# An FFT kernel's opening stage: folding the first batch in place, and lining up TensorE's work on it

## The chip, the cores and the metric

The kernel runs on one core of a Trainium2 chip. The metric is the device time of one execution in microseconds (us), the median of several runs. A core has TensorE (PE; its weight loads are shown apart, as PEld), VectorE (DVE), ScalarE (ACT), GpSimd (POOL) and SyncE (SP). Transfers between the chip's memory and the core's are issued from SP, ACT or POOL and carried by 16 DMA engines.

## The reference

A two-dimensional Fourier transform whose real part is kept, and then a feed-forward layer with the hardswish gate, all in float32:

```
x: (8, 3008, 256)                      # batch, sequence, dimension
X = fft(fft(x, axis=1), axis=2).real   # -> (24064, 256)
h = X @ w_in                           # w_in:  (256, 2048)
g = h * clip(h + 3, 0, 6) / 6
out = g @ w_out                        # w_out: (2048, 256)
```

## The kernel before

The sequence length is 3008 = 47 x 64. The transform over it is done in two stages: a transform over 47 points by matmuls with the table F (stage 1), a trip through device memory that regroups the rows (tiles z, zd and g), and a transform over 64 points by matmuls with the table T (stage 2). The transform over the dimension is folded into w_in. The inner transform uses symmetry: for a real input it needs only the sums and the differences of column d and column 256 - d ("near" and "far" columns, 127 of each; columns 0 and 128 stand alone). Making these sums and differences is the *fold*.

The eight batches are worked in four pairs. For all but the first batch, stage 1 hides beside the feed-forward layer's matmuls, which fill TensorE. The first batch (halves[0], "hb" in the code) has nothing to hide beside: it makes the opening of the kernel, the first 40 us or so, in which the weights are also loaded and split into exponent and mantissa (lines 778 to 818).

The order on each engine is the order in which the program issues its instructions (the schedule is written out by hand); the engines run apart and meet at semaphores. For the first batch that order is as follows.

- **Loads.** SP loads the first piece of w_in (load_w(0), L757). ACT issues F, FI (a table of identities and indices) and the rows of the special slot n2 = 0, which go into a tile first_slot (L196). POOL issues eight gathers (L175), 128 rows of 4 KB each: for each of four groups of slots, m in FIRST = [0, 1, 3, 2], a tile x and its mirrored partner xr, each one *unit* of 4 slots x 256 columns on partitions 0 to 46 and 64 to 110. Behind them on POOL's queue stand C (L934), a part of T (L865) and two pieces of w_out (load_w(2) and (3), L762).
- **Fillers.** keep_awake(n, w) (L871) issues n matmuls of 128 rows x w columns on a zeroed tile Z, whose product nobody reads. Four of 512 columns run first, one of 128 columns stands ahead of the first unit, and one of 128 columns follows each of units 2 to 6 (L961).
- **Units.** For each unit, fold_unit (L201) makes a tile y from the pool ypool, which has two buffers: the edge columns 0 and 128 are copied (L205, on ACT for most units, on DVE for the first and the last), DVE makes the differences (L207) and the sums (L208). Then unit_columns (L332) does four matmuls of 512 columns, one for each quarter of the array (47 x 64 weights each: two halves of rows by two halves of columns, running side by side), and unit_middle (L326) does eight small products of one or two columns for the middle column 128. A float32 matmul stands in the trace as two records, one for each of its passes. In the group m = 3 one quarter takes the special slot by other tables ("alone"), which makes three matmuls of the one; the special slot's rows are copied into the tile x by ACT (L967) first.
- **Evictions.** When both units of a group are accumulated in PSUM, evict_first (L348) copies them into a tile z: the middle columns (L353) and the first half (L354) on ACT, the second half (L355) on ACT for the first two groups and on DVE for the last two. SP (and ACT, for one half of the last group) then issues the DMAs to zd (L367). In the program's order the eviction of one group stands behind the first unit of the next. Behind the first of them SP issues load_w(1), the second piece of w_in.
- **The last unit.** Its fold is done in two steps of two slots each, and its columns in two rounds of four matmuls of 256 columns. DVE's join(0) (L812), which completes the first piece of w_in, is issued behind them, and so is the third group's eviction ahead of them.
- **After the units.** fold_w_in(0) (wps, L848) waits for join(0) and C; the last group is evicted; load_g_half (L435) brings zd back as g; exponent_a(1) and mantissa(1) (L778, L803, L804) wait for load_w(1), exponent_b(1) (ex, L792) follows on TensorE and exponent_c(1) (L795) on ACT, then join(1), fold_w_in(1), and stage 2 (L455). From about 46 us on the feed-forward layer's matmuls fill TensorE.

The clearing of the table T by ACT (clear_table, L904) and the first piece's exponent (L778, L792, L795) run ahead of the units.

Of the kernel before, what the change touches and what calls it, by code (L numbers as in the profile page):

```python
# [7 lines left out]
F32 = mybir.dt.float32  # L8
# [5 lines left out]
AL = mybir.AluOpType  # L14
# [35 lines left out]
N1, N2 = 47, 64  # L50
# [8 lines left out]
def kernel(  # L59
# [10 lines left out]
    nc = tc.nc  # L70
    P = nc.NUM_PARTITIONS
    B, S, D = x.shape
# [6 lines left out]
    PB, PZ = P // 2, 2 * NK1  # L79
    PX = PB + N1 + 1  # L80
    XC = 4
    NS = N2 // 2
    NXC = NS // XC
    NM = NXC // 2
# [13 lines left out]
    ypool = ctx.enter_context(tc.tile_pool(name="ypool", bufs=2))  # L98
# [41 lines left out]
    FIRST = [0, 1, NM - 1, 2]  # L140
# [54 lines left out]
    def load_zero(o, hb, queue):  # L195
        queue.dma_start(out=o, in_=x_pn[hb.b * N1:(hb.b + 1) * N1 + 1, 0, :])  # L196

    def zero_slot(hb):
        return hb.x[NM - 1][PB:PX, XC - 1, :]

    def fold_unit(x, part, steps=(slice(0, XC),), copy=nc.scalar.copy, sine=nc.vector):  # L201
        y = ypool.tile([PX - 1, XC + 1, D], F32, tag="y", name="y")
        n = PX - 1
        for js in steps:
            copy(y[:, js, 0:P + 1:P], x[0:n, js, 0:P + 1:P])  # L205
            far, near = x[0:n, js, D - 1:P:-1], x[0:n, js, 1:P]
            sine.tensor_tensor(y[:, js, P + 1:D], *((far, near) if part else (near, far)), op=AL.subtract)  # L207
            nc.vector.tensor_tensor(y[:, js, 1:P], near, far, op=AL.add)  # L208
        return y

    def fold_half(hb, m, part, eng):
        xt, xr = hb.x[m][0:PX - 1], hb.xr[m][0:PX - 1]
# [90 lines left out]
    def rows(b):  # L303
        return slice(b * PB, b * PB + N1)

    def table(i, b):
        return F[rows(b), i * PB:(i + 1) * PB]
# [8 lines left out]
    def quarters(m, part):  # L316
        for i in range(2):
            for h in range(2):
                alone = m == NM - 1 and h == i == 1
                a = (2 * i, XC - 1 - 2 * i)[part]  # L320
                n = 1 if alone else 2
                yield i, h, slice(0, n), slice(a, a + n) if part == 0 else slice(a, a - n if a >= n else None, -1), False
                if alone:
                    yield i, h, slice(1, 2), slice(XC - 1, XC) if part == 0 else slice(0, 1), True

    def unit_middle(m, part, x, pt):  # L326
        for i, h, js, slots, alone in quarters(m, part):
            t = (1 + part) if alone else (5, 7)[part]
            nc.tensor.matmul(pt[h][i * PB:(i + 1) * PB, js], table(t, h), x[rows(h), slots, P:P + 1],
                             start=part == 0 and not alone, stop=part == 1, skip_group_check=True)  # L330

    def unit_columns(m, part, y, ps, only=None):  # L332
        def product(o, t, h, moving, begin):
            nc.tensor.matmul(o, table(t, h), moving, start=begin, stop=bool(part), skip_group_check=True)  # L334

        for i, h, js, slots, alone in quarters(m, part):
            o = ps[h][i * PB:(i + 1) * PB]
            if alone and only in (None, 1):
                for k, cs in enumerate((slice(0, P + 1), slice(P + 1, D))):
                    product(o[:, js, cs], 1 + part + 2 * k, h, y[rows(h), slots, cs], False)  # L340
            elif not alone and only is None:
                product(o[:, js], (0, 6)[part], h, y[rows(h), slots], part == 0)
            elif not alone:
                for j, slot in zip(range(js.start, js.stop), range(XC)[slots]):
                    if j == only:
                        product(o[:, j:j + 1], (0, 6)[part], h, y[rows(h), slot:slot + 1], False)

    def evict_first(hb, m, ps, pt):  # L348
        k = FIRST.index(m)
        pool, tag = ((zpool, "z"), (zpool, "z"), (apool, "a"), (cpool, "c"))[k]  # L350
        z = pool.tile([PX, 2, 2, D + 1], F32, tag=tag, name="z")
        for h in range(2):
            nc.scalar.copy(z[:, h, :, D:], pt[h][0:PX])  # L353
        nc.scalar.copy(z[:, 0, :, 0:D], ps[0][0:PX])  # L354
        (nc.vector.tensor_copy if k > 1 else nc.scalar.copy)(z[:, 1, :, 0:D], ps[1][0:PX])  # L355
        if not first.zd:
            first.zd[0] = dpool.tile([NG, 2 * KK, 2, NS, D + 1], F32, tag="zd0", name="zd")
        zd = first.zd[0][:].rearrange("g k c (h n) d -> (g k c) h (n d)", h=2)
        n0 = 2 * 4 * KK
        for i in range(2):  # L360
            n = (m * XC + 2 * i) * (D + 1)
            for j in range(PZ // n0):
                dst = zd[j * n0:(j + 1) * n0, :, n:n + 2 * (D + 1)]
                rs = slice(i * PB + j, i * PB + 2 * n0, 2) if j < 2 else slice(i * PB + 2 * n0, i * PB + PZ)
                src = z[rs].rearrange("p h n d -> p h (n d)")
                if j == 0:
                    (nc.scalar if k == NM - 1 and i else nc.sync).dma_start(out=dst, in_=src)  # L367
                else:
                    later.setdefault((j, k), []).append((dst, src))
# [404 lines left out]
    def exponent_a(j, signs=range(2)):  # L774
        top = raw[j][:].bitcast(I16).rearrange("p (n four) -> p n four", four=4)[:, :, 3]
        for i in signs:
            low = PM[j % len(PM)][:, i].bitcast(U8).rearrange("p (n two) -> p n two", two=2)[:, :, 0]
            nc.scalar.activation(low, top, AF.Identity, bias=bias[:, i:i + 1], scale=(1 - 2 * i) / 16.0)  # L778
# [15 lines left out]
    def exponent_c(j):  # L794
        nc.scalar.activation(exs[j].bitcast(I32), exs[j], AF.Identity, scale=2.0 ** 23)  # L795
# [11 lines left out]
    def join(j):  # L807
        kind, n, i = PIECES[j]
        frac, ex = fracs.pop(j), exs.pop(j)
        if kind == "in":  # L810
            o = wpool.tile([P, WB], F32, tag="wi", bufs=4, name="wi")
            nc.vector.tensor_tensor(o[:], frac, ex, op=AL.mult)  # L812
            w[PIECES[j]] = o[:]
            return

        for h, g in enumerate((B21, B22) if i else (B11, B12)):
            f, e = (t.rearrange("p (c q h e) -> h p c q e", c=2, h=2, e=DH)[h] for t in (frac, ex))
            nc.vector.tensor_tensor(block(n, g).rearrange("p c (q e) -> p c q e", e=DH), f, e, op=AL.mult)

    def block(j, i):  # L820
        return G[:, i, 2 * j:2 * j + 2, :]
# [49 lines left out]
    def keep_awake(n, w=2 * TB):  # L871
        ps = ps_d.tile([P, 2 * TB], F32, tag="d", name="awake")
        for i in range(n):
            nc.tensor.matmul(ps[:, 0:w], ones[:], Z[:, 0:w], start=True, stop=True)
# [5 lines left out]
    hb = halves[0]  # L880
# [1 line left out]
    nc.scalar.dma_start(out=F[:], in_=c_stage1[:, 0:8 * PB])  # L882
    nc.scalar.dma_start(out=FI[:], in_=c_stage1[:, 13 * PB:])
    first_slot = qpool.tile([P, 2 * TB], F32, tag="qn", name="first_slot")
    load_zero(first_slot[PB:PX, 0:D], hb, nc.scalar)
    for k, m in enumerate(FIRST):
        take_half(hb, m, *((xpool, "x"), (xpool, "x"), (qpool, "q"), (apool, "a"))[k])
    bias = wpool.tile([P, 2], F32, tag="bias", name="bias")
# [12 lines left out]
    def clear_table(b):  # L901
        r = slice((1 - b) * N2, (2 - b) * N2)
        t = T[r, b].rearrange("p g a k n -> p g (a k n)")
        nc.scalar.copy(t, Z[r].unsqueeze(1).to_broadcast([N2, NG, 2 * TB]))  # L904
# [31 lines left out]
    for j in range(2, 4):  # L936
        load_w(j)
    clear_table(0)
    exponent_a(0)
    mantissa(0)  # L940
    exponent_b(0)
    keep_awake(1, P)
    clear_table(1)
    for k, m in enumerate(FIRST):
        ps, pt = first_banks(m)
        end = k == NM - 1
        for part, tiles in enumerate((hb.x, hb.xr)):
            x = tiles.pop(m)
            if end and part:
                y = fold_unit(x, 1, (slice(1, XC, 2), slice(0, XC, 2)), copy=nc.vector.tensor_copy)  # L950
                evict_first(hb, FIRST[k - 1], *before)
                unit_middle(m, 1, x, pt)
                for j in range(2):
                    unit_columns(m, 1, y, ps, only=j)
                join(0)
                continue
            y = fold_unit(x, part, copy=nc.scalar.copy if k + part else nc.vector.tensor_copy)
            unit_columns(m, part, y, ps)
            unit_middle(m, part, x, pt)
            if k + part and not end:  # L960
                keep_awake(1, P)  # L961
            if k == part == 0:
                exponent_c(0)
            if part == 0 and k > 0 and not end:
                evict_first(hb, FIRST[k - 1], *before)
            if k == 1 and part == 0:
                nc.scalar.copy(zero_slot(hb), first_slot[PB:PX, 0:D])  # L967
                load_w(1)
        before = ps, pt
    evict_first(hb, m, *before)  # L970
    load_g_half(hb, 0)
# [110 lines left out]
    ps = spare[0]  # L1082
# [198 lines left out]
```

## Time and profile before

| | |
|---|---|
| median of 3 runs | 1941.01 us (1940.43 to 1942.53) |
| the profiled execution | 1940.9 us |
| its span | 1939.1 us |
| TensorE busy in the span | 1921.7 us (99%) |
| mean granted TensorE clock | 0.994 |

The profile is of one execution; the span runs from its first instruction to its last, and 1.8 us lie around it. The page gives the busy time of each engine, the span in 40 slices, the chain of work that ended last and the costliest groups. Since the change touches the first tens of microseconds, the views that matter are those of stretches of time: the engines' busy time and the granted clock (PEclk) by stretch, and the timeline, whose rows give the start, the time covered by a merged group, the engine, the line, the tiles written and read, the number of records, and in brackets the engine's idle time before them and what ended it.

### The profile page before, as it was taken

To read this page: it belongs to the slowest core of one execution; us is meant where nothing else is said; L and a number is where in the kernel's file an instruction comes from. 1 tells how busy PE (TensorE), PEld (TensorE's weight loads), DVE (VectorE), ACT (ScalarE), POOL (GpSimd) and SP (SyncE) were. 2 spreads that over 40 slices of the span, in tenths; PEclk is the share of its full clock that TensorE was granted. 3 is DMA by queue.
4 is the path that set the end of the run, shared out by engine and by line. 5 is a ranking of instruction groups with operands and counts; after the bars stand their busy time and mean duration, and the time that the engine had idled before them with its cause. 6 is when DMAs were issued, how large, how long until landed. Compare 5 with 4: busy or idle time off the path is not lost.

```text
span 1939.1 us, 28192 instructions
## 1 busy us (share of the span) xinstructions
PE 1921.7 (99%) x9336; PEld 1655.2 (85%) x9336; DVE 1428.7 (74%) x2756; ACT 679.3 (35%) x1169; POOL 1442.8 (74%) x1653
## 2 busy tenths in 40 slices
PE   8999999999999999999999999999999999999998
PEld 5678888888988888888898888888899888888887
DVE  5877776777777777777787777777778777777777
ACT  5633333333333333333333333333333333333332
POOL 4586888887678877787678887878667667666765
PEclk7999999999999999999999999999999999999999
DMA  7522222311112222111111221112110101101000
GB/s 243 163 80 55 50 73 69 81 45 31 38 33 50 59 73 55 44 50 32 37 36 46 56 55 44 50 52 52 36 28 20 28 17 26 31 17 28 18 21 20
DMA packets 155592, 99.03 MB, mean 51 GB/s; under 512 B 122163, under 2 KB 137246, under 8 KB 155446
## 3 DMA queue, kind: packets, MB, share of 16 engines
q1 hardware_dynamic: 142982, 58.07, 12.4%
q0 software_dynamic: 11168, 38.51, 6.8%
q8 instruction: 73, 1.20, 0.3%
q10 hardware_dynamic: 1296, 0.66, 0.1%
q14 instruction: 73, 0.60, 0.1%
HBM read 59.87 MB, written 37.32 MB: 50 GB/s over the span
## 4 chain that ended last, share of the span: by engine, by line
PE 95%; DVE 2%; ACT 1%; POOL 1%; issue 0%; DMA 0%; ACTq 0%; DVEq 0%; SPq 0%; POOLq 0%
PE acc L649 55%; PE v L554 16%; PE u L554 16%; PE ps L502 2%; PE acc L629 1%; PE ps L281 1%; DVE a L605 1%; PE ps L334 1%; PE spare L848 1%; DVE s L563 0%; ACT t L602 0%; POOL c L619 0%; DVE o L710 0%; DVE u L586 0%; PE ps L463 0%
## 5 line engine op out<-in xcount | busy, mean ns | idle before, releaser
L619 POOL TENSOR_TENSOR c<-a 128x512 f32<-128x512 f32 (+1 forms) x375 | 469.2, 1251 | 360.7 <-PE acc L649 312.7
L649 PE MATMUL acc<-c,G 128*128 128x256 f32 (+1 forms) x3008 | 697.3, 375 | 0.1
L602 ACT ACTIVATE t<-u,half 128x512 f32<-128x512 f32 (+1 forms) x384 | 260.6, 679 | 1143.9 <-DVE u L573 1064.6
L649 PEld LDWEIGHTS acc<-c,G 128*128 128x128 f32 x3008 | 565.1, 190 | 72.0 <-POOL c L619 1.0
L563 DVE SCALAR_TENSOR_TENSOR s<-qn,WN,u 128x256 f32<-128x256 f32 (+1 forms) x768 | 330.6, 472 | 340.6 <-PE u L554 340.3
L649 PE MATMUL acc<-a,G 128*128 128x256 f32 (+1 forms) x2256 | 541.6, 376 | 0.0
L649 PEld LDWEIGHTS acc<-a,G 128*128 128x128 f32 x2256 | 421.0, 189 | 73.6 <-issue 20.2
L554 PE MATMUL v<-q,W 127*128 127x256 f32 (+1 forms) x1536 | 389.2, 375 | 1.6 <-DVE a L605 1.6
L554 PE MATMUL u<-q,W 128*128 128x256 f32 (+1 forms) x1536 | 387.9, 375 | 0.0
L605 DVE SCALAR_TENSOR_TENSOR a<-t,u 128x512 f32<-128x512 f32 (+2 forms) x448 | 264.1, 601 | 100.7 <-ACT t L602 97.6
L554 PEld LDWEIGHTS v<-q,W 127*128 127x128 f32 x1536 | 288.1, 190 | 41.9 <-DVE a L605 1.9
L554 PEld LDWEIGHTS u<-q,W 128*128 128x128 f32 x1536 | 285.8, 190 | 36.9 <-issue 2.4
L619 POOL TENSOR_TENSOR c<-a,c 128x256 f32<-128x256 f32 (+1 forms) x375 | 268.5, 716 | 29.4
L619 POOL TENSOR_TENSOR c<-c,a 128x256 f32<-128x256 f32 (+1 forms) x375 | 268.4, 716 | 29.4
L573 DVE TENSOR_TENSOR u<-s,v 128x512 f32<-128x512 f32 x352 | 245.0, 696 | 37.4 <-DVE s L563 0.9
L605 DVE SCALAR_TENSOR_TENSOR a<-t,v 128x512 f32<-128x512 f32 (+1 forms) x480 | 263.7, 566 | 0.1
L602 ACT ACTIVATE t<-v,half 128x512 f32<-128x512 f32 (+1 forms) x384 | 260.5, 678 | 0.2 <-issue 0.2
L575 DVE TENSOR_TENSOR v<-v,s 128x512 f32<-128x512 f32 x352 | 243.9, 693 | 0.0
L619 POOL TENSOR_TENSOR r<-w,e 128x256 f32<-128x256 f32 (+1 forms) x92 | 88.7, 985 | 3.6
L659 ACT ACTIVATE e<-acc 128x512 f32<-128x512 f32 (+2 forms) x184 | 83.3, 544 | 0.0
L710 DVE STREAM_TRANSPOSE o<-r 128x256 f32<-128x256 f32 (+1 forms) x192 | 72.5, 415 | 0.2
L619 POOL TENSOR_TENSOR w<-w,e 128x512 f32<-128x512 f32 (+1 forms) x46 | 57.5, 1250 | 3.6
(120 smaller groups left out, 786.1 us busy)
## 6 DMA issues: line engine op xcount, KB each, us to landing
out_dram<-o SPq DMA_DIRECT2D x744, 32.0 KB
g<-zd SPq DMA_DIRECT2D x42, 256.0 KB
zd<-z SPq DMA_DIRECT2D x48, 192.0 KB
xt<-in_x_dram POOLq DMA_DIRECT2D x21, 256.0 KB, 3.8
st<-in_moe_w_out_dram POOLq DMA_DIRECT2D x8, 512.0 KB, 7.1
qn<-qd SPq DMA_DIRECT2D x16, 256.0 KB
xt<-in_x_dram POOLq DMA_DIRECT2D x17, 192.0 KB, 4.1
st<-in_moe_w_in_dram POOLq DMA_DIRECT2D x6, 512.0 KB, 7.6
```

What stands on the lines that cost most here:

```text
L281: nc.tensor.matmul(ps[b][h * PB:(h + 1) * PB, 0:n], F[rows(b), 0:PB], y[rows(b), 2 * h:2 * h + n], start=True, stop=not last, skip_group_c ...
L502: nc.tensor.matmul(ps[:, blk, u * P:n].rearrange("p (b k) -> p b k", b=2), g[:, kk, blk * (P + 1):blk * (P + 1) + P], T[:, :, gr, blk, kk, ...
L554: nc.tensor.matmul(ps[:, i, 0:nq], W1[r, blk, f * P:(f + 1) * P], q[r, blk, of:of + nq], start=True, stop=True)
L563: nc.vector.scalar_tensor_tensor(s[:, i, 0:nq], qn[:, of:of + nq], WN[:, f:f + 1], u[:, i, 0:nq], op0=AL.mult, op1=AL.add)
L573: nc.vector.tensor_tensor(u[:], s[:], v[:], op=AL.add)
L575: nc.vector.tensor_tensor(v[:], v[:], s[:], op=AL.subtract)
L602: nc.scalar.activation(t, h, AF.Relu, bias=half[:], scale=scale)
L605: nc.vector.scalar_tensor_tensor(dst, t, 1.0, h, op0=AL.min, op1=AL.mult)
L619: (eng or nc.gpsimd).tensor_tensor(out, in0, in1, op=AL.add)
L649: nc.tensor.matmul(ch.acc[i // 2][:, i % 2, 0:ch.n], G[:, i, fc, :], mv, start=(fc == 0 and i % 2 == 0), stop=(fc == NF - 1), skip_group_c ...
L659: nc.scalar.mul(ch.e[:, k:i + 1, 0:ch.n], ch.acc[i // 2][:, 0:i + 1 - k, 0:ch.n], 1.0 / WS)
L710: nc.vector.transpose(o[:, 0:n // DH, h], ch.r[:, m, h, 0:n].rearrange("p (j i) -> p j i", i=DH))
```

## The change

- fold_unit is replaced by fold_columns, which folds in place: near becomes near + far, and then far becomes that sum minus twice the old far (or its negative for the partner tiles), by a scalar_tensor_tensor that reads the first instruction's result. There is no tile y and no copy of the edge columns; all the folds stand in a row on DVE, ahead of TensorE's loop in the program's order, the last unit again in two steps, and join(0) behind them.
- The special slot is folded on its own in first_slot (two instructions of 48 x 127, ahead of the first piece's mantissa on DVE) and is read from there; its copy into x is gone.
- Each quarter's matmul of 512 columns becomes two: one of 2 x 129 columns over columns 0 to 128, and one of 2 x 127 columns over the far columns, which are read backwards. The first of each unit waits only for the sums, the second for the differences.
- The middle products of both units of a group stand together between the two units' columns.
- The filler ahead of the first unit becomes two of 512 columns; the five fillers between the units are gone.
- A group's eviction is still issued behind the next group's first unit. The second half's copy is on ACT for the first three groups and on DVE for the last.

```diff
-    def fold_unit(x, part, steps=(slice(0, XC),), copy=nc.scalar.copy, sine=nc.vector):
-        y = ypool.tile([PX - 1, XC + 1, D], F32, tag="y", name="y")
-        n = PX - 1
-        for js in steps:
-            copy(y[:, js, 0:P + 1:P], x[0:n, js, 0:P + 1:P])
-            far, near = x[0:n, js, D - 1:P:-1], x[0:n, js, 1:P]
-            sine.tensor_tensor(y[:, js, P + 1:D], *((far, near) if part else (near, far)), op=AL.subtract)
-            nc.vector.tensor_tensor(y[:, js, 1:P], near, far, op=AL.add)
-        return y
+    def fold_columns(x, part, eng):
+        near, far = x[:, :, 1:P], x[:, :, D - 1:P:-1]
+        eng.tensor_tensor(near, near, far, op=AL.add)
+        eng.scalar_tensor_tensor(far, far, (-2.0, 2.0)[part], near, op0=AL.mult, op1=(AL.add, AL.subtract)[part])
...
+    def unit_source(x, part, h, slots, alone):
+        return zero.unsqueeze(1)[0:N1] if alone and part == 0 else x[rows(h), slots]
...
+    def unit_columns(m, part, x, ps, only=None):
+        for k, (to, fr) in enumerate([(slice(0, P + 1), slice(0, P + 1)), (slice(P + 1, D), slice(D - 1, P, -1))]):
+            for i, h, js, slots, alone in quarters(m, part):
...
+                t = (1 + part + 2 * k) if alone else (0, 6)[part]
+                nc.tensor.matmul(ps[h][i * PB:(i + 1) * PB, js, to], table(t, h),
+                                 unit_source(x, part, h, slots, alone)[:, :, fr],
+                                 start=part == k == 0 and not alone, stop=part == 1, skip_group_check=True)
...
-        (nc.vector.tensor_copy if k > 1 else nc.scalar.copy)(z[:, 1, :, 0:D], ps[1][0:PX])
+        (nc.vector.tensor_copy if k == NM - 1 else nc.scalar.copy)(z[:, 1, :, 0:D], ps[1][0:PX])
...
+    fold_columns(zero.unsqueeze(1), 0, nc.vector)
     exponent_a(0)
     mantissa(0)
     exponent_b(0)
-    keep_awake(1, P)
+    keep_awake(2)
     clear_table(1)
+    exponent_c(0)
+    for k, m in enumerate(FIRST):
+        for part, tiles in enumerate((hb.x, hb.xr)):
+            late = k == NM - 1 and part
+            for js in (slice(1, XC, 2), slice(0, XC, 2)) if late else (slice(0, XC),):
+                fold_columns(tiles[m][0:PX - 1, js], part, nc.vector)
+    join(0)
     for k, m in enumerate(FIRST):
         ps, pt = first_banks(m)
-        end = k == NM - 1
-        for part, tiles in enumerate((hb.x, hb.xr)):
-            x = tiles.pop(m)
-            if end and part:
-                y = fold_unit(x, 1, (slice(1, XC, 2), slice(0, XC, 2)), copy=nc.vector.tensor_copy)
-                evict_first(hb, FIRST[k - 1], *before)
-                unit_middle(m, 1, x, pt)
-                for j in range(2):
-                    unit_columns(m, 1, y, ps, only=j)
-                join(0)
-                continue
-            y = fold_unit(x, part, copy=nc.scalar.copy if k + part else nc.vector.tensor_copy)
-            unit_columns(m, part, y, ps)
-            unit_middle(m, part, x, pt)
-            if k + part and not end:
-                keep_awake(1, P)
-            if k == part == 0:
-                exponent_c(0)
-            if part == 0 and k > 0 and not end:
-                evict_first(hb, FIRST[k - 1], *before)
-            if k == 1 and part == 0:
-                nc.scalar.copy(zero_slot(hb), first_slot[PB:PX, 0:D])
-                load_w(1)
+        x, xn = hb.x.pop(m), hb.xr.pop(m)
+        unit_columns(m, 0, x, ps)
+        if k > 0:
+            evict_first(hb, FIRST[k - 1], *before)
+        if k == 1:
+            load_w(1)
+        unit_middle(m, 0, x, pt)
+        unit_middle(m, 1, xn, pt)
+        for j in range(2) if k == NM - 1 else (None,):
+            unit_columns(m, 1, xn, ps, j)
         before = ps, pt
     evict_first(hb, m, *before)
```

More of the change, by code (lines that the diff above doesn't have):

```diff
@@ L328, in unit_middle @@
             t = (1 + part) if alone else (5, 7)[part]
-            nc.tensor.matmul(pt[h][i * PB:(i + 1) * PB, js], table(t, h), x[rows(h), slots, P:P + 1],
+            nc.tensor.matmul(pt[h][i * PB:(i + 1) * PB, js], table(t, h),
+                             unit_source(x, part, h, slots, alone)[:, :, P:P + 1],
                              start=part == 0 and not alone, stop=part == 1, skip_group_check=True)
[L332 to L346, printed above, removed]
+    def unit_columns(m, part, x, ps, only=None):
+        for k, (to, fr) in enumerate([(slice(0, P + 1), slice(0, P + 1)), (slice(P + 1, D), slice(D - 1, P, -1))]):
+            for i, h, js, slots, alone in quarters(m, part):
+                if only is not None:
+                    js, slots = range(XC)[js], range(XC)[slots]
+                    if only not in js:
+                        continue
+                    slot = slots[js.index(only)]
+                    js, slots = slice(only, only + 1), slice(slot, slot + 1)
+                t = (1 + part + 2 * k) if alone else (0, 6)[part]
+                nc.tensor.matmul(ps[h][i * PB:(i + 1) * PB, js, to], table(t, h),
+                                 unit_source(x, part, h, slots, alone)[:, :, fr],
+                                 start=part == k == 0 and not alone, stop=part == 1, skip_group_check=True)
     def evict_first(hb, m, ps, pt):
@@ L884 @@
     first_slot = qpool.tile([P, 2 * TB], F32, tag="qn", name="first_slot")
[L885 removed]
+    zero = first_slot[PB:PX, 0:D]
+    load_zero(zero, hb, nc.scalar)
     for k, m in enumerate(FIRST):
```

## The prediction

> **What bounds the kernel now.** The page comes first. TensorE is full in all but the first of the 40 slices, and only there is the granted clock below full: whatever a change of the opening can give lies in those 48 us.
>
> ```profile
> PE   8999999999999999999999999999999999999998
> PEclk7999999999999999999999999999999999999999
> ```
>
> Next, the busy time by stretch, cut where the granted clock changes or was kept (columns: stretch, its length, busy us and records of PE, PEld, DVE, ACT, POOL, then clock, DMA share, GB/s).
>
> ```profile
> 1.65:5.06 3.41, 3.41 (x4) 1.47 (x5) 1.44 (x3) 2.88 (x2) 2.69 (x5) 1.00 0.98 281
> 5.06:11.88 6.82, 4.99 (x35) 2.02 (x37) 5.04 (x9) 5.93 (x7) 5.30 (x6) 1.00 0.99 368
> 11.89:18.71 6.82, 5.59 (x44) 2.61 (x40) 2.57 (x4) 1.91 (x7) 4.19 (x6) 0.50 0.99 319
> 18.71:25.53 6.82, 6.22 (x60) 4.86 (x52) 2.66 (x6) 1.50 (x6) 0.00 (x0) 0.50 0.84 270
> 28.95:32.36 3.41, 3.41 (x27) 2.14 (x24) 1.36 (x3) 0.98 (x4) 0.00 (x0) 0.50 0.16 39
> 32.37:39.19 6.82, 6.14 (x31) 4.50 (x30) 4.66 (x9) 5.50 (x9) 2.93 (x6) 1.00 0.50 135
> 39.20:46.01 6.81, 5.65 (x31) 4.68 (x30) 5.15 (x12) 3.84 (x8) 4.73 (x6) 1.00 1.01 335
> ```
>
> And the group of middle products in 5.06 to 31:
>
> ```profile
> L329 PE MATMUL pt<-xt,F 47*64 47x2 f32 (+1 forms) x68 | 3.1, 224 | 0.3 <-ACT z L353 0.3
> ```
>
> The clock is full to 11.89, half to 32.37, and full again. The edges lie 6.83 us apart or a multiple of it. A stretch with TensorE busy 4.99 of 6.82 us (73%) ended in a drop; one with 5.65 of 6.81 (83%) didn't. The way up took a stretch of 3.41 us wholly filled by long matmuls. 18.71 to 25.53 is 91% busy by the records and brought no rise, but many of its 60 records are middle products of one or two columns (68 of them in all), which stream little.
>
> Third, the timeline of the units, at full and at half clock.
>
> ```profile
> 8.96 1.09 PE L334 MATMUL ps<-y,F 47*64 47x512 f32 x8 [0.65 <-DVE y L208]
> 12.13 0.80 PE L874 MATMUL awake<-Z,ones 128*128 128x128 f32 x2
> 16.66 0.69 DVE L207 TENSOR_TENSOR y<-xt 111x508 f32<-111x508 f32 x1 [3.18 <-ACT xt L967]
> 16.91 1.99 PE L334 MATMUL ps<-y,F 47*64 47x512 f32 x8 [1.23 <-ACT y L205]
> 18.67 0.34 PE L329 MATMUL pt<-xt,F 47*64 47x2 f32 x8
> 28.86 2.02 PE L334 MATMUL ps<-y,F 47*64 47x256 f32 x16
> 30.81 2.74 PE L848 MATMUL wps<-wi,C 128*128 128x256 f32 x8
> ```
>
> A unit costs 1.09 us at full clock and 1.99 at half, a filler 0.80, and ACT's edge copies and the slot's copy hold TensorE and DVE up. So the eight units end at 28.86 + 2.02 = 30.9. From there the path runs on as follows.
>
> ```profile
> 32.50 2.07 ACT L778 ACTIVATE PM<-st,bias 128x512 uint8<-128x512 int16 x3 [0.99 <-DVE top L803]
> 33.39 1.02 PE L874 MATMUL awake<-Z,ones 128*128 128x512 f32 x2
> 34.25 0.59 PE L792 MATMUL ex<-PM,FI 128*128 128x512 f16 x2
> 36.39 1.89 PE L848 MATMUL wps<-wi,C 128*128 128x256 f32 x8
> 38.11 0.38 PE L455 MATMUL ps<-T,g 128*128 128x128 f32 x2
> ```
>
> Stage 2 starts at 38.11: 5.61 us behind the second weight piece's exponent (32.50), and behind the first product wps. I take the start of stage 2 as the mark: what it moves by, the rest should move by, since the loads that follow are released by this same chain.
>
> **The change part by part.**
>
> *Fold.* Rows for DVE:
>
> ```profile
> 6.08 0.43 DVE L803 TENSOR_SCALAR top<-st 128x512 int32<-128x512 int32 x1 [2.88 <-DMA st<-in_moe_w_in_dram]
> 6.54 0.69 DVE L804 SCALAR_TENSOR_TENSOR top<-st,top 128x512 f32<-128x512 uint32 x1
> L207 DVE TENSOR_TENSOR y<-xt 111x508 f32<-111x508 f32 x7 | 4.8, 687 | 6.5 <-ACT xt L967 3.2 <-issue 2.6 <-DMA xt<-in_x_dram,IT 0.3
> L207 DVE TENSOR_TENSOR y<-xt 111x254 f32<-111x254 f32 x2 | 0.8, 417 | 0.0
> 7.54 0.18 DVE L205 COPY y<-xt 111x8 f32<-111x8 f32 x1 [0.31 <-DMA xt<-in_x_dram,IT]
> L812 DVE TENSOR_TENSOR wi<-top,ex 128x512 f32<-128x512 f32 x1 | 0.7, 677 | 0.0
> ```
>
> The sum stays 0.69. The second instruction is of L804's kind (0.69) and now reads the first: L803 to L804 shows that such a wait adds 0.03. A unit's fold is 0.69 + 0.69 + 0.03 = 1.41, and the last, in two steps, 4 x 0.42 plus gaps, 1.75. The special slot's pair (48 x 127) has no row: between 2 x 0.18 (L205) and 2 x 0.42 (L207's half form), taken at 0.5. It waits for first_slot and pushes the mantissa (done at 7.23) to about 7.75, 0.2 behind the first landing at 7.54: hidden by the fillers below. The folds wait for nothing but gathers:
>
> ```profile
> 1.69 1.12 POOL L175 DMA_INDIRECT xt<-in_x_dram,IT  x1 [0.54 <-POOL IT L926]
> 11.61 1.08 POOL L175 DMA_INDIRECT xt<-in_x_dram,IT  x1 [0.30 <-issue]
> DMA to landing us min/median/max: 6.1/6.1/6.4
> ```
>
> (Eight are issued, these are the first and the last.) With up to 6.4 us from issue to landing the last gather is there at 18.0, and they come (11.61 - 1.69) / 7 = 1.42 apart on average, the fold's own pace. So DVE ends the seventh fold near 17.6, the last at 18.0 + 1.75 = 19.75, and join(0) at 20.45.
>
> *TensorE.*
>
> ```profile
> 7.93 0.38 PE L874 MATMUL awake<-Z,ones 128*128 128x128 f32 x2
> ```
>
> Two fillers of 512 columns (1.02 for one, tail included) run from 7.93 to about 9.7, where one of 128 ended at 8.3; the first unit starts 0.7 later, which costs nothing, since the last fold decides. Five fillers of 0.80 go. A unit keeps its 512 columns (1.09 at full clock) in twice the matmuls; with 0.34 or less of middle products it stays near the fold's 1.41. Reading columns backwards has no row on TensorE. It could gain nothing, since the columns are the same, and cost at most another pass's time, 0.5 per unit; I take zero, as DVE reads the same columns backwards at its forward rate (L207's 687 ns for 508 elements beside L812's 677 for 512). The eight units then end near 20.2 instead of 30.9, and wps(0) runs from 20.5 to 22.4 at full clock.
>
> *Clock.* By 11.89 TensorE has run fillers, two exponent products, two long fillers and two units with gaps of some 0.4 us in all: over 90% busy, above the 83% that kept the clock. I expect it to stay full there. From 11.89 to 18.71 it waits for folds: five units of 1.09 and eight groups of middle products of 0.2 give about 6.2 us by the records, some 4.8 us (70%) of real streaming, between the case that dropped and the one that kept: open.
>
> *Evictions.* ACT takes one more copy (0.6) and loses seven small ones; it idles in this stretch (1.91 busy of 6.82), so nothing. DVE's third copy goes from between the folds. SP issues the first eviction about 13 instead of 16.23, and load_w(1) right behind it, past nothing else.
>
> *What is late next: load_w(1).* SP issued the eviction and load_w(1) from 16.23 to 18.8, but from 18 to 21 only POOL's queue moved data, and theirs came from 21.5 on; at 25.54 all is landed.
>
> ```profile
> 16.23 1.34 SPq L367 DMA_DIRECT2D zd<-z  x2
> 17.61 1.17 SPq L757 DMA_DIRECT2D st<-in_moe_w_in_dram  x2
> q0 software_dynamic: 255, 0.86, 100.0%
> q1 hardware_dynamic: 722, 0.76, 59.4%
> 25.54:28.95 3.41, 3.15 (x31) 1.62 (x31) 2.66 (x8) 0.54 (x3) 0.00 (x0) 0.50 0.00 0
> ```
>
> (q0 is POOL's queue in 18 to 21, q1 SP's in 21.5 to 25.5.) Transfers seem served in the order in which they arrive. All that was moved by 25.5 must still move, and the DMA share is 0.99 to 18.7: load_w(1) lands between 22.5 (served with w_out's pieces) and 25.4 (as before). I take 24.6. Before, it had long landed at 32.50; now it is the wait.
>
> **Sum.** The exponent of piece 1 starts at 24.6 instead of 32.50: 7.9 earlier, and stage 2 with it at full clock (30.2). The other way into stage 2, the last eviction and g, took 38.11 - 30.9 = 7.2 from the last unit: 27.4, or 29.4 behind the queue, not last. But TensorE has little to do between 22.4 and about 25.4; at 25.54 (the edges lie where they lay) the stretch behind is some 60% busy, and the clock likely drops. Then wps(1) and the next exponent product take 1.9 + 0.4 us longer: stage 2 moves by 5.6. Of 5.6 and 7.9 I take 6.3, nearer the lower. Against the profiled 1940.9: 1934.6. The median shown, 1941.01, is 0.1 from that, so the forecast stands for the median too.
>
> **A rule against a row.** The records show a drop at 11.89 with no idle gap over 1 us in the 6.8 us before it. The Trainium skill, "TensorE: Matmul & The Clock Gate", section "What's actually happening", has the clock fall after at least one idle window of about 3.4 us; the trace disagrees, since a window 73% busy was enough. By the rule nothing would drop here.
>
> **Rivals.**
>
> 1. *The clock never drops in the opening* (the gaps stay below what counts): the full 7.9, 1933.0. For: the stretch at 83% kept it. Against: the stretch at 73% lost it. The page just named would have it so.
> 2. *Earlier transfers slow the gathers.* The eviction and load_w(1), 0.64 MB, share the engines with the last gathers: at 368 GB/s the last lands 1.7 later, and all behind it: 1936.3. Against: in 18 to 21 SP's data got no share. The Trainium skill, "DMA: Bandwidth & Descriptors", section "Queues, rings and completion order", says that an engine takes turns between queues packet by packet, which would do this; the rows for 18 to 21 speak against it.
> 3. *A drop given back later.* The opening's later part (39.20 to 46.01, 83% busy) loses a little density as it moves, ends in a drop, and the clock is back a stretch of 6.83 us later: at half clock that is 3.4 us of lost work, 1934.6 + 3.4 = 1938.0.
> 4. *Slower: the clock stays half without the fillers.* It drops at 18.71 and no stretch of 3.41 us is filled before TensorE's work becomes dense at 46, as each waits for a load. Price: 6.14 + 5.65 = 11.8 us of the stretches 32.37 to 46.01 run twice as long, of which their idle time takes up at most 13.63 - 11.8 = 1.8: 10 longer, less the 5.6 gained, 1945.3. It decides if no window before about 40 is filled. Against: at half clock the same work fills windows the more easily, as 28.95 to 32.36 shows.
> 5. *It does not do what it says*: the clock drops at 11.89 all the same. Six units at half clock, 1.76 from start to start (16.91 to 18.67) and 0.3 of middle products, end at 24.2. By the way over g stage 2 starts at 24.2 + 7.2 = 31.4, and as wps(1) too runs at half clock 1.9 later, 33.3: 4.8 gained, 1936.1.
>
> **How the numbers follow.** Chances: forecast 0.45; rival 1 0.22; rival 2 0.10; rival 3 0.11; rival 4 0.06; rival 5 0.06. Of all, 0.2% (3.9 us, about what a measurement can tell from no change) is passed by the forecast and rivals 1, 2 and 5, less a few hundredths for their edges: faster 0.80. Rival 3 and those edges: same 0.13. Rival 4 and a little of rival 3: slower 0.07. The range goes from 1931.6 (7.9 gained and 1.4 more if load_w(1) comes at 23) to 1938.2 (rival 3); rival 4 and the tails are left out.
>
> **What would show it.** PEclk full past 11.89; DVE's last fold near 19.8 with idle time before it given to a gather; the last unit near 20.2; PM's second run (L775 in the new file) started by a landing near 24.6; stage 2's first product between 30 and 33. Wrong would be: a fold pair well over 1.41, gathers landing after 18.5, or half clock beyond 36.

## The result, and the profile after

| | before | changed |
|---|---|---|
| median of 9 runs | 1940.54 us | 1933.56 us |
| lowest to highest | 1939.69 to 1942.62 | 1932.08 to 1937.56 |
| ratio, with its 95% interval | 1 | 0.9967 (0.9956 to 0.9977) |
| the profiled execution, its span | 1940.9, 1939.1 | 1932.08, 1930.3 |

The changed kernel is 7 us faster, a third of a per cent. Its nine executions are spread over 5.5 us, and that spread turned out to be a part of the answer. The profile is of the fastest of the nine. Its page shows the granted clock full in the first slice too:

```profile
PEclk9999999999999999999999999999999999999999
```

The stretches are cut here where this execution's clock has its edges (columns as in the prediction: the stretch, its length, busy us and records of PE, PEld, DVE, ACT and POOL, then clock, DMA share, GB/s):

```profile
7.31:14.13 6.82, 6.03 (x66) 3.10 (x68) 6.51 (x11) 3.80 (x6) 5.91 (x8) 1.00 1.01 394
14.14:20.96 6.82, 6.82 (x173) 6.28 (x165) 6.06 (x11) 4.45 (x13) 1.44 (x2) 1.00 1.02 341
20.97:27.78 6.81, 3.93 (x16) 2.12 (x15) 3.74 (x8) 3.84 (x7) 0.36 (x2) 1.00 0.58 187
27.79:34.60 6.81, 6.81 (x43) 6.16 (x42) 4.37 (x10) 2.89 (x8) 6.34 (x9) 1.00 0.87 252
```

DVE is full while it folds (6.51 and 6.06 of 6.82 us, where it had 2.57 from 11.89 to 18.71 before). From 20.97 to 27.78 TensorE is busy 58% of the time: that is the new wait. The timeline shows what it waits for. These are the changed kernel's fold (the first unit, the start of the second, the first step of the last), the end of the units, and the way to stage 2:

```profile
7.84 0.68 DVE L203 TENSOR_TENSOR xt<-xt 111x508 f32<-111x508 f32 x1
8.55 0.69 DVE L204 SCALAR_TENSOR_TENSOR xt<-xt 111x508 f32<-111x508 f32 x1
9.38 0.69 DVE L203 TENSOR_TENSOR xt<-xt 111x508 f32<-111x508 f32 x1
17.46 0.42 DVE L203 TENSOR_TENSOR xt<-xt 111x254 f32<-111x254 f32 x1
19.06 1.10 PE L341 MATMUL ps<-xt,F 47*64 47x129 f32 x29
20.09 1.99 PE L845 MATMUL wps<-wi,C 128*128 128x256 f32 x8
23.94 2.08 ACT L775 ACTIVATE PM<-st,bias 128x512 uint8<-128x512 int16 x3 [3.20 <-DMA st<-in_moe_w_in_dram]
27.45 1.96 PE L845 MATMUL wps<-wi,C 128*128 128x256 f32 x8
29.24 0.94 PE L452 MATMUL ps<-T,g 128*128 128x128 f32 x7
```

The units end at 19.06 + 1.10 = 20.2, not 30.9. ACT then waits 3.20 us for load_w(1), to 23.94, and stage 2 starts at 29.24, not 38.11: 8.9 earlier, and the span is 8.8 shorter. Stage 2's start is a good mark: in all fourteen profiles of this study, the span is 1901.0 to 1901.5 us longer than the time of that start.

### The profile page after: what moved, and what is told of

It reads as the page before. It is cut to its first block, busy times and chain, and to the rows that moved or that the text cites. A ratio compares the mean times of both kernels' runs of the same rounds, so it can differ in the third digit from the quotient of the medians.

```text
span 1930.3 us, 28293 instructions
## 1 busy us (share of the span) xinstructions
PE 1913.4 (99%) x9400; PEld 1652.3 (86%) x9400; DVE 1427.6 (74%) x2754; ACT 679.2 (35%) x1163; POOL 1444.4 (75%) x1653
## 4 chain that ended last, share of the span: by engine, by line
PE 95%; DVE 3%; ACT 1%; issue 0%; DMA 0%; SPq 0%; DVEq 0%; ACTq 0%
PE acc L646 57%; PE v L551 16%; PE u L551 16%; PE ps L499 2%; PE ps L276 1%; PE acc L626 1%; DVE a L602 1%; ACT t L599 0%; DVE s L560 0%; PE awake L871 0%; PE spare L845 0%; DMA st<-in_moe_w_in_dram 0%; DVE o L707 0%; DVE u L583 0%; PE ps L460 0%
```

## The clock falls in some executions and not in others

The two profiles differ before any changed instruction has run (the first, the special slot's fold, starts at 6.02). This is the first row of TensorE in the timeline, before and changed, with the same four fillers:

```profile
1.61 5.40 PE L874 MATMUL awake<-Z,ones 128*128 128x512 f32 x8 [1.61 <-DVE ones L878]
```

```profile
1.61 6.51 PE L871 MATMUL awake<-Z,ones 128*128 128x512 f32 x8 [1.61 <-DVE ones L875]
8.39 1.88 PE L871 MATMUL awake<-Z,ones 128*128 128x512 f32 x4
```

Both start at 1.61, but the same eight records take 5.40 us before and 6.51 here. The third row shows why: at full clock a record of this kind takes some 0.47 us (1.88 for four), while these took 0.68 and 0.81 on average. The opening starts at half clock, and the clock rose at 5.06 there and at 7.31 here. (The profile's records of the clock only begin with that rise, so a view of an earlier stretch shows 1.00 all the same. The prediction's "full to 11.89" should be full from 5.06 to 11.89.) In the fourteen profiles of this study the clock rose anywhere from 4.75 to 7.67. The edges of the clock's stretches thus lie elsewhere in each profile, while their length is fixed: every interval between two changes of the clock is a multiple of 3.41 us. The Trainium skill, "TensorE: Matmul & The Clock Gate", section "What's actually happening", says that this window is free-running and 3413 ns long; the traces agree.

So a kernel has no single time here, but a set of them, and an execution's mean granted clock tells which. As an estimate from the profiles, whose tails lie at half clock for 2.1 to 5.2 us: at 0.999 there is hardly more than the tail, at 0.998 a stretch of 3.4 us more (6.8 at most), at 0.995 or less one of some 14 us or more. Before, in the 61 executions beside the experiments, it was 0.993 to 0.997: it always fell, and the time goes with it, from 1942.6 us at 0.993 to 1936.4 at 0.997. That the place of the edges decides which time an execution gets fits all this, but isn't shown, since there is only one profile of each kernel. The changed kernel's nine:

| mean clock | executions | us |
|---|---|---|
| 0.999 | 2 | 1932.08, 1932.28 |
| 0.998 | 4 | 1933.45, 1933.47, 1933.56, 1935.34 |
| 0.995 | 3 | 1936.16, 1936.32, 1937.56 |

The medians below are read together with these counts. "Held" means 0.998 or more.

## The experiments

Theory A: the gain is the waits for ACT's copies, gone. Theory B: it is the clock, held by the long fillers. After the first four runs I formed theory C: the waits and the fillers act through the same thing, a clock that falls when TensorE's work is thin, so that neither part alone does much.

Each ratio below is to the kernel before as it ran beside that experiment. Its medians there were 1938.94 us (experiments 1, 2, 3 and 9), 1940.46 (4, 5, 7 and the first of 6) and 1940.52 (8, 10, 11 and the second of 6).

**1 (e1). The changed kernel with the old fillers.**

```diff
-    keep_awake(2)
+    keep_awake(1, P)
...
+        if 0 < k < NM - 1:
+            keep_awake(1, P)
...
+        if k < NM - 1:
+            keep_awake(1, P)
```

> The changed kernel with the fillers of before: one of 128 columns ahead of the first unit and one behind each of units 2 to 6. Theory A (the gain is the waits for ACT's edge copies, gone): the folds still run at the gathers' pace, the eight units still end by about 21 to 23, and at least two thirds of the gain stays: about 1934 to 1936. Theory B (the gain is the clock, which the long fillers hold at full): the clock falls near 12 us as before, two units at full clock, six at about 2.05 us and four fillers of 0.80 end near 26 or later, and at most 3 of the 7 us stay: 1937.5 to 1940.

Measured: 1941.06 us, ratio 1.0 (0.9986 to 1.0013), no gain. But the twelve executions fall into two heaps: three held the clock, at 1932.5 to 1933.4, and nine didn't, at 1940.3 to 1942.1. The profile of one of the nine:

```profile
8.17:11.57 3.40, 2.98 (x46) 1.15 (x44) 3.30 (x6) 2.60 (x2) 2.53 (x3) 1.00 1.02 401
11.58:14.99 3.41, 2.31 (x22) 1.13 (x22) 3.34 (x6) 1.26 (x4) 3.41 (x6) 1.00 1.01 411
15.00:32.05 17.05, 17.05 (x175) 12.74 (x172) 6.09 (x12) 4.82 (x14) 0.45 (x1) 0.50 0.53 171
```

DVE folds at full pace to 15, and still the clock falls there; then TensorE, at half clock and with fillers at double length, is never idle for 17 us. As the cause of the median, theory A falls: the waits are gone, and nine of twelve executions gained nothing. Where the clock held, the old fillers cost nothing that can be told: 1932.5 to 1933.4, against 1932.08 and 1932.28.

**2 (e2). The kernel before with the new fillers alone.**

```diff
-    keep_awake(1, P)
+    keep_awake(2)
...
-            if k + part and not end:
-                keep_awake(1, P)
```

> The kernel before with only the fillers changed: two of 512 columns ahead of the first unit, none between the units. Theory A: DVE and TensorE still wait for ACT's copies behind the evictions, the gaps are still there, the clock falls or not, and the units end between 26 and 29: 1938 to 1941. Theory B: the clock stays full past 12 us, units cost 1.09 instead of 1.99, the units end by 24: 1934 to 1937.

Measured: 1938.72 us, ratio 0.9994 (0.9985 to 1.0003); none of eleven held. With long fillers ahead the clock falls later, and the waits for ACT leave TensorE 76% and then 52% busy just before:

```profile
11.08:14.48 3.40, 2.58 (x44) 1.18 (x36) 2.22 (x4) 0.50 (x4) 3.10 (x6) 1.00 1.02 416
14.49:17.90 3.41, 1.78 (x26) 1.01 (x30) 2.20 (x4) 1.61 (x5) 1.27 (x2) 1.00 1.05 383
17.91:31.55 13.64, 12.10 (x92) 8.50 (x85) 7.22 (x17) 5.05 (x15) 0.00 (x0) 0.50 0.51 159
```

Theory B in its plain form falls too: these fillers alone hold nothing. The median lies in theory A's range, 1938 to 1941.

**3 (e3). The kernel before with the copies on DVE.**

```diff
-            y = fold_unit(x, part, copy=nc.scalar.copy if k + part else nc.vector.tensor_copy)
+            y = fold_unit(x, part, copy=nc.vector.tensor_copy)
...
-                nc.scalar.copy(zero_slot(hb), first_slot[PB:PX, 0:D])
+                nc.vector.tensor_copy(zero_slot(hb), first_slot[PB:PX, 0:D])
```

> The kernel before with only the edge columns' and the special slot's copies moved from ACT to DVE (0.18 us each there); fold, order and fillers as before. Theory A: the waits for ACT (2.7 us of TensorE, 3.2 of DVE) go, and with them a third or more of the gain: 1936 to 1938.5. Theory B: the clock falls near 12 us all the same and the units at half clock with their fillers decide: 1939.5 to 1941.

Measured: 1937.98 us, ratio 0.9989 (0.9979 to 0.9998). Three of twelve held, at 1932.9 to 1933.4: the changed kernel's own time, with the folds still made into y. The other nine lie at 1937.7 to 1939.3. Theory A's range, 1936 to 1938.5, has the median in it, but it foresaw one time and not two.

**4 (e6). The short filler ahead, none between.** Of the changed kernel:

```diff
-    keep_awake(2)
+    keep_awake(1, P)
     clear_table(1)
```

> The changed kernel with the short filler of before (128 columns) ahead of the first unit, and none between the units. Theory C (the two parts only work together: the clock falls unless two stretches of 3.41 us in a row are dense enough, so the folds without waits and the long filler are both needed): the stretch around 8 to 15 is thin again, the clock falls in most executions and the units run at half clock, but without the five fillers: 1936 to 1939, with single executions near 1932.5 where it stays. Theory A (the waits alone): 1933 to 1934, as the changed kernel.

Measured: 1934.84 us, ratio 0.9971 (0.9961 to 0.9982); four of eight held. Against experiment 1 only the five short fillers between the units are gone, and that is worth some 6 us of median: the range that theory C gave (1936 to 1939) was too slow. Most of this lies in the executions that lost the clock, 1935.4 to 1937.2 here and 1940.3 to 1942.1 there; five fillers of 0.80 us at half clock make 4.0 of it. Whether the short fillers also made the clock fall more often (nine of twelve there, four of eight here) so few executions can't tell. A 128-column filler is thin work, by an estimate: the row of 7.93 in the prediction has 0.38 us for it, in which its two passes stream 2 x 0.11, a quarter of the 0.43 of a pass of 512 columns. The profile shows a short drop, in the wait for load_w(1):

```profile
22.59:25.99 3.40, 1.04 (x4) 0.27 (x3) 1.56 (x3) 1.60 (x3) 0.00 (x0) 1.00 0.48 159
26.01:29.40 3.39, 3.33 (x9) 1.93 (x9) 2.79 (x6) 3.37 (x6) 1.52 (x4) 0.50 0.56 156
29.42:32.80 3.38, 3.38 (x23) 3.04 (x22) 1.35 (x3) 1.24 (x5) 3.38 (x5) 1.00 0.86 228
```

One stretch at 31% busy, then one at half clock, and full again. Stage 2 starts at 30.46, against 29.24.

**5 (e7). Long fillers ahead, and the five between kept.** Of experiment 1's kernel:

```diff
-    keep_awake(1, P)
+    keep_awake(2)
     clear_table(1)
```

> The changed kernel with its two long fillers ahead of the first unit and, besides, the five fillers of 128 columns between the units. Theory C: the stretches get denser, the clock stays full in nearly all executions, five fillers of 0.4 us at full clock cost little, since TensorE waits for the folds anyway: 1932.5 to 1934.5, with fewer executions above 1935 than the changed kernel has. Rival (the fillers between the units are what the old kernel lost by): 1936 to 1940.

Measured: 1933.28 us, ratio 0.9960 (0.9946 to 0.9973), all five within 0.44 us and all held. With the long fillers ahead the five short ones cost little here: they move the start of wps from 20.09 to 22.90, but most of that hides in the wait for load_w(1), and stage 2 starts at 29.84, against 29.24.

**6 (e8 and e12). Folds into y, copies on DVE, new fillers.** Both diffs of experiments 2 and 3 together; nothing is folded in place.

> The kernel before with its folds into y, but the edge and slot copies on DVE, and with the changed kernel's fillers (two of 512 columns first, none between). Nothing is folded in place and no matmul is split. Theory C: as the waits for ACT are gone and the long filler is there, the clock stays full in most executions and load_w(1) decides: 1933 to 1935, the changed kernel's time. Theory D (in-place folds are needed for the pace): units end 2 us or more later, 1936 to 1938.

Measured: 1936.07 us, ratio 0.9970 (0.9959 to 0.9981). Two of seven held, at 1932.94 and 1934.84; five lie at 0.995 or 0.996. The same with the five short fillers kept, which is experiment 3's kernel with

```diff
-    keep_awake(1, P)
+    keep_awake(2)
     clear_table(1)
```

> The kernel before with its folds into y, the edge and slot copies on DVE, two fillers of 512 columns first and the five short fillers kept: e8 with the short fillers back, to hold the clock as they did with the folds in place. Theory C: the clock stays full in most executions, and the folds into y then cost as little as those in place: 1932.8 to 1934. Theory D (the folds in place are worth time by themselves): all executions at 1935 or more, at full clock too.

Measured: 1937.89 us, ratio 0.9981 (0.9972 to 0.9991). Four of eleven held, at 1932.5 to 1933.3, and seven lie at 1937.8 or more. So at full clock the folds into y are as good as those in place, and theory D's 1935 falls. Theory C's "most executions" was wrong both times, and the first median lies in theory D's range (1936 to 1938), though by the clock and not by the pace of the folds. The folds into y hold the clock less often: 4 of 11, where experiment 5 with the same fillers held in 5 of 5. In the profile of the first of these two kernels TensorE is thin just ahead of the drop at 16.03:

```profile
12.62:16.02 3.40, 1.83 (x27) 0.71 (x22) 2.63 (x7) 1.20 (x4) 3.25 (x5) 1.00 1.00 365
```

**7 (e9). The kernel before, all its waits kept, with dense fillers.**

```diff
-    keep_awake(1, P)
+    keep_awake(2)
...
-                keep_awake(1, P)
+                keep_awake(1)
```

> The kernel before with all its waits for ACT, but with denser fillers: two of 512 columns first and one of 512 columns (0.86 us at full clock) behind each of units 2 to 6. Theory C: the fillers fill the waits, the clock stays full in most executions, a unit with its filler takes about 2.2 us at full clock instead of 2.8 to 3.6, and the units end near 26 to 27 instead of 30.9: 1935.5 to 1937.5. Theory A (the waits cost the time and the clock is incidental): the fillers only add work, 1939 to 1943.

Measured: 1935.68 us, ratio 0.9976 (0.9966 to 0.9987), eight executions within 0.44 us, all at 0.999. This is the cleanest separation of the study: nothing but fillers was added, every wait for ACT stands, and the clock that they hold gives 4.8 us net of their own work, where the whole change gives 7. It also shows that fillers alone can hold the clock, if there are enough of them: experiment 2 has the same two ahead, but none between the units. The timeline still shows a wait for ACT:

```profile
16.43 1.09 PE L334 MATMUL ps<-y,F 47*64 47x512 f32 x8 [0.93 <-ACT y L205]
17.51 1.13 PE L874 MATMUL awake<-Z,ones 128*128 128x512 f32 x2
```

The waits and the added filler work together cost 1935.68 - 1932.2 = 3.5 us against the changed kernel's two executions at 0.999.

**8 (e5). More filler in the wait for load_w(1).** Of the changed kernel:

```diff
     exponent_a(1)
-    keep_awake(1)
+    keep_awake(3)
     exponent_b(1)
```

> The changed kernel with three fillers of 512 columns instead of one behind the first product wps, where TensorE waits for load_w(1) from about 22.9 to 24.7. Theory F (the executions of the changed kernel near 1936 to 1937.6, 3 of 9, lost the clock in this wait): none above 1935.5 now. Rival G (they lost it among the units, where TensorE waits for folds): about a third still near 1936 to 1938.

Measured: 1932.59 us, ratio 0.9959 (0.9945 to 0.9973), five executions within 0.44 us, all at 0.999. That is as theory F expected. It doesn't settle it: at the changed kernel's rate of 3 in 9 above 1935.5, five without one would come up about one time in eight, and experiment 5, which left this wait alone, had none either. Both make the opening denser, at different places.

**9 (e4). load_w(1) earlier.** In the changed kernel, POOL issues it behind the last gather, ahead of C.

```diff
-                (nc.gpsimd if j > 1 else nc.sync).dma_start(
+                (nc.gpsimd if j > 0 else nc.sync).dma_start(
...
+    load_w(1)
     nc.gpsimd.dma_start(out=C[:], in_=c_dim.rearrange("(h p) d -> p h d", p=P))
...
-        if k == 1:
-            load_w(1)
```

> The changed kernel with load_w(1) issued by POOL right behind the last gather, ahead of C, instead of by SP behind the first eviction. In the changed kernel TensorE and ACT wait for it to 23.9. Theory (load_w(1) is what is late): it lands near 19, the exponent of piece 1 starts when ACT is free at about 21, and stage 2 starts 1 to 1.5 us earlier, until the last eviction and its way over g bind: 1932 to 1932.7 against 1933.6 for the changed kernel. Rival (the way of the last eviction over zd and g ends as late, or C, T and the w_out pieces come later and hold the products): no gain, 1933.4 to 1934.5.

Measured: 1931.42 us, ratio 0.9961 (0.9948 to 0.9975), four of five at 0.999. The first exponent then waits only for DVE, but C comes late, and stage 2 waits for g:

```profile
21.08 1.97 PE L845 MATMUL wps<-wi,C 128*128 128x256 f32 x8 [0.44 <-DMA C<-in_c_dim_dram]
25.89 1.89 PE L845 MATMUL wps<-wi,C 128*128 128x256 f32 x8
28.94 1.13 PE L452 MATMUL ps<-T,g 128*128 128x128 f32 x8 [1.17 <-DMA g<-zd]
```

So load_w(1) was what was late, as the theory said: the second wps now ends at 27.78, where it ended at 29.41. But the way over g is next, only 0.3 us below: stage 2 starts at 28.94 instead of 29.24, not 1 to 1.5 earlier. The median is below the range of either. That the clock falls less often, since the wait is shorter, may be a part of it; the four executions that held at 0.999 (1930.4 to 1931.7) are faster than the changed kernel's two as well.

**10 (e10). load_w(1) early, load_w(3) late.** Of the changed kernel:

```diff
-    def load_w(j):
+    def load_w(j, queue=nc.gpsimd):
...
-                (nc.gpsimd if j > 1 else nc.sync).dma_start(
+                (nc.gpsimd if j > 0 else nc.sync).dma_start(
...
-            nc.gpsimd.dma_start(out=o.rearrange("p (c j) -> p c j", c=2),
+            queue.dma_start(out=o.rearrange("p (c j) -> p c j", c=2),
...
     nc.gpsimd.dma_start(out=C[:], in_=c_dim.rearrange("(h p) d -> p h d", p=P))
+    load_w(1)
     load_t(0, queue=nc.gpsimd)
-    for j in range(2, 4):
-        load_w(j)
+    load_w(2)
...
-        if k == 1:
-            load_w(1)
...
     evict_first(hb, m, *before)
+    load_w(3, nc.sync)
```

> The changed kernel with the transfers reordered: POOL issues gathers, C, load_w(1), T, load_w(2); load_w(3) goes to SP's queue behind the last group's eviction. In e4 the last eviction's transfer took 4.3 us behind the w_out pieces, and C came 0.4 late. If transfers are served in order of arrival, zd lands 1.3 us or more earlier and wps starts without a wait: stage 2 starts near 27.5 to 28 instead of 28.9, 1929 to 1930.7 where the clock stays full. Rival (load_w(3) is now late for its exponent, or the way over g is bound by fixed times of the transfers): 1931 to 1932.5.

Measured: 1931.15 us, ratio 0.9953 (0.9939 to 0.9966), all five at 0.999. That median lies in the rival's range (1931 to 1932.5), and only the fastest execution, the profiled one at 1930.66, in the theory's. There stage 2 starts at 27.90, as expected for the last eviction's earlier landing:

```profile
27.90 1.13 PE L452 MATMUL ps<-T,g 128*128 128x128 f32 x8 [0.16 <-DMA g<-zd]
```

It is the best version of the study, 2.4 us below the changed kernel's median and 1.0 below its executions at 0.999. Experiment 9's median isn't told apart from it.

**11 (e11). The same with the five short fillers.** The lines that experiment 1 adds, added to experiment 10's kernel:

```diff
+        if 0 < k < NM - 1:
+            keep_awake(1, P)
...
+        if k < NM - 1:
+            keep_awake(1, P)
```

> e10 with the five short fillers between the units. If these hold the clock as in e7, no execution is more than 1 us above the lowest, at e10's best or up to 0.8 above it for the fillers' own time: 1929.3 to 1931.2. Rival (without the idle time that e7 had, the fillers delay the units): 1931.5 or more.

Measured: 1933.15 us, ratio 0.9962 (0.9949 to 0.9976), all five at 0.999: steady, but the rival was right. Once nothing waits for load_w(1), the fillers' own time counts: wps starts at 22.96 instead of 20.29, much as in experiment 5, and this time stage 2 moves with it, to 30.81 from 27.90.

## Why the prediction was right, point by point

The forecast was 1934.6 and the median is 1933.56; what the kernel does was read rightly in most steps, and one step was wrong in kind. That the median came so near is in part luck: it is the middle of a mixture that the prediction did not foresee.

- **Fold.** Right: a pair of instructions takes 0.71 + 0.69 (1.41 was said), and successive units overlap by 0.1. The gathers landed a little earlier: the last fold starts at 17.46, not 18.0, as soon as DVE is free.
- **TensorE.** Right: the units end at 20.2 (20.2), and wps runs from 20.09 to 22.08 (20.5 to 22.4). Reading columns backwards costs nothing here: a unit's sixteen records, 2 x 129 and then 2 x 127 columns, take 1.09 us as eight of 512 did.

```profile
10.20 1.09 PE L341 MATMUL ps<-xt,F 47*64 47x258 f32 x16
```

- **load_w(1).** Right, and the heart of it: it lands at 23.94 (24.6 taken, 22.5 to 25.4 as bounds). Experiment 9 shows that it was the wait. It was issued later than forecast, though: the first eviction went out at 15.13 and not at about 13, and load_w(1) behind it at 16.51. That cost nothing that shows, because POOL's queue was still being served: from 17.5 to 20 it carried 205 of 214 packets, as it would in a service by order of arrival.

```profile
16.51 1.83 SPq L754 DMA_DIRECT2D st<-in_moe_w_in_dram  x2
q0 software_dynamic: 205, 0.72, 94.0%
q1 hardware_dynamic: 9, 0.01, 1.4%
```

  Rival 2 didn't happen: the last gather had landed by 17.46. The Trainium skill's turns between queues, "DMA: Bandwidth & Descriptors", section "Queues, rings and completion order", don't show in these rows.
- **Clock: the step that failed.** I wrote that "the edges lie where they lay" and so gave the changed kernel one fate, a drop at 25.54. The edges lie elsewhere in each profile, and several cases are there in the nine executions. By their mean clocks 1932.08 and 1932.28 hardly lost it (rival 1 said 1933.0; in the profile load_w(1) landed 0.66 us earlier than taken, and stage 2 followed 5.30 behind it instead of 5.61). Four lost some 3.4 us, which is the forecast's case: experiment 4's profile shows such a drop in this wait, at 26.00, and there it moves stage 2 by 1.2 us and not by 2.3. Three lost about 14 us and lie near rival 5's 1936.1, but no profile shows where. The mistake was to take the edges of the one profile of before for a property of the kernel. The share of 73% or 83% busy over 6.83 us didn't sort the cases either. The clock's intervals are multiples of 3.41 us, and cut so, the 73% are 85% and then 61%; the changed kernel kept its clock through two stretches of 58%. One sum is off as written, too: five units of 1.09 and eight groups of 0.2 make 7.05 us, not 6.2. With 0.91 from a unit's start to its middle products they do make 6.2, and the profile has 6.03 busy there.
- **What made the gain.** The prediction gave it to the waits and the fillers side by side. Experiment 7 shows that most of it (4.8 us of 7) can be had from the clock, and experiments 1 and 2 that neither the change's folds nor its fillers by themselves give its median.
- **Rivals 3 and 4 (a drop given back later, and slower without fillers).** None of the nine executions comes to their 1938.0 and 1945.3; the slowest has 1937.56.

What stays open is the rule by which the clock falls. It takes thin work, but the busy share of the records doesn't tell how thin: 87% and 68% in a row lost it in experiment 1, two stretches of 58% didn't in the changed kernel. Nor does the longest gap: TensorE was never idle for more than 0.85 us at a time in the 6.83 us ahead of the drop in the profile of before, and the changed kernel kept its clock over a gap of 1.81. The former stretches were mostly matmuls on quarters of the array, the latter whole ones; that quarters count for less is a guess that no run here tests.

## What to carry to other kernels

Before a gain in a short opening is explained or predicted, look at the spread of single executions and their mean granted clock: one profile shows one position of the clock's window, and the kernel's time may be a choice between two. A filler that keeps TensorE awake should be wide and stand in time that is idle anyway; here seven of 512 columns held the clock in every execution, and narrow ones between the units cost the most where the clock had fallen. When a stage is pulled forward, the next thing late is a transfer whose place in the queue was never important before, so look up where each of the following loads stands in it.

## What the runs showed of the hardware that I had not expected

- The same instructions give 1932.5 or 1942.1 us (experiment 1), with a mean granted clock of 0.999 or 0.993; the clock's window of 3.41 us lies elsewhere in each profile.
- A drop doesn't need an idle window: the clock fell after stretches that were 68% (experiment 1) and 52% busy (experiment 2).
- Seven fillers of 512 columns that compute nothing, put into an otherwise unchanged kernel in the place of short ones, made it 4.8 us faster and cut its spread from 6.2 us to 0.44 (experiment 7).
